# Attention scores turned by VectorE block transposes in place of TensorE transposes

## The chip, the cores and the metric

One Trainium2 chip, of which the kernel uses one core. The metric is the device time of the program in microseconds. Engines are named as in the profile: PE is TensorE (PEld its weight loads), DVE is VectorE, ACT is ScalarE, POOL is GpSimd, SP is the queue that issues the DMAs.

## The reference, cut to what matters

Three parts follow one another. Attention packs 576 keys of each of 64 heads (8 batches of 8 heads) into 32 vectors and lets 576 queries attend to them; a gated feed-forward layer with an RMS norm follows, then a second feed-forward layer with h·cos(h).

```python
def sm_attn(qq, kk, vv):
    s = scale * np.matmul(qq, kk.transpose(0, 1, 3, 2))
    s = s - np.max(s, axis=-1, keepdims=True)
    a = np.exp(s)
    a = a / (np.sum(a, axis=-1, keepdims=True) + 1e-09)
    return np.matmul(a, vv)
p_packed = sm_attn(p, k, v)              # 32 packed vectors of each head
out = sm_attn(q, p_packed, p_packed)     # 576 queries, 32 keys: the softmax that the change rebuilds
# then: x = rows (batch, position), 512 columns
xn = x / rms * rms_g
g = xn @ w_gate; x1 = (silu(g) * (xn @ w_val)) @ w_out     # d_ff 1536
h = x1 @ w_in;   y = (h * cos(h)) @ w2_out                 # d_ff 2048
```

All of it is float32. The kernel keeps the precision by splitting each operand of the large matmuls into a high and a low part (`hilo`) and adding three products (`mm3`).

## The kernel before, in words

**First stage.** A loop over i from 0 to 17 packs one group of four heads per pass: `u_prep`, `u_kt`, `u_s1`, `u_e`, `u_et`, `u_pp`, `u_fin`, while the weights are loaded and turned from 64-bit to 32-bit form (`narrow`: DVE lines 143 to 153 on tiles wy, ny). From pass 5 on the attention of batch 0 runs in it: `attend(0)` is a generator and `bg0_step` takes three of its steps per pass, until `ATT_U` steps are done.

**Blocks.** Then come eight blocks, one per batch b, of 24 iterations each (12 column groups f of the first feed-forward layer, two halves of the positions). An iteration is `gv_block` (12 matmuls into two PSUM tiles named gv), a step of attention, `acc_block` (6 matmuls into acc, for the iteration three before), another step of attention, and at six places `unit` (8 matmuls into mps, then `hilo`). `acc_block` has a place in its middle where only steps whose name begins with x are taken. In block b the steps of `attend(b+1)` are spread by `att_step`: `N_ATT` steps over the 48 half-iterations. So blocks 0 to 6 hold the attention of batches 1 to 7, and block 7 none. Block 0 also narrows the rest of the weights (`b0_step`), which loads DVE, ACT and POOL more than in later blocks.

**Attention of one batch before.** For each of two head groups g: query tiles (96 positions, 2 heads, 6 chunks) are transposed on PE three at a time into a PSUM tile qtp, ACT copies it to qT; after four of these, 8 matmuls give the scores sp, two tiles of 128 rows (4 heads by 32 keys) by 288 positions. ACT and DVE copy one each to sT, six PE transposes bring positions to the rows (stp, 96 rows), DVE takes the maximum over 32 keys and subtracts it into s. Then two exponentials on ACT (line 264), two sums, reciprocals and products on DVE (268 to 274). The steps named in `ATT_ORD` follow: t (three PE transposes into atp, ACT copies to at), x (matmuls xp with the packed vectors, squares for the norm on ACT, sums on DVE), r (rp, the root), b (the root is broadcast by three PE transposes into rb and multiplied into at), p (`hilo` into apt, the operand of `gv_block`).

**Order and buffers.** From the first stage until well into the last one the program order is the order in which the code is written (`manual_schedule`), on every engine. PSUM tiles of attention, `unit` and gv share one pool: two banks in the first stage, four in the blocks, taken in turn. An engine executes its instructions in order, so a wait holds all that stands behind it.

**Last stage.** The second feed-forward layer (`h_block`, `o_block`) has no attention in it; `o_out` stores the rows.

Of the kernel before, what the change touches and what calls it, by code (L numbers as in the profile page):

```python
# [20 lines left out]
def kernel(  # L21
# [14 lines left out]
    nc = tc.nc  # L36
    B, H, S, D = q.shape
    NP = p.shape[2]
# [3 lines left out]
    CP = 96  # L42
    NC_ = S // CP
    HALF = S // 2
    CH = NC_ // 2
# [7 lines left out]
    scale = 1.0 / math.sqrt(D)  # L53
# [30 lines left out]
    ATT_FROM, ATT_TO, ATT_FROM0, ATT_TO0, N_ATT = 0, 48, 10, 45, 37  # L84
    BX, BS, BW = 10, 13, 12

    wide = w_gate.dtype != F32
# [89 lines left out]
    psb = [ps_bg]  # L177
# [38 lines left out]
        nc.sync.dma_start(out=cl, in_=c_dram[b])  # L216

    def attend(b):
        s = a1.tile([CP, NC_, H, NP], F32, tag="s", name="s")
        for g in range(2):  # L220
            qTs = []
            for j in (2 * g, 2 * g + 1):
                qv = qn.pop(4 * b + j)
                qT = a2.tile([128, 2, HALF], F32, tag="qT", name="qT")
                for i in range(2):
                    tp = psb[0].tile([128, HALF], F32, tag="mm", name="qtp")
                    for c in range(CH):
                        nc.tensor.transpose(  # L228
                            tp[:, c * CP:(c + 1) * CP], qv[:, i, 2 * c:2 * c + 2, :].rearrange("p c d -> p (c d)"),
                            ident[:CP, :CP],  # L230
                        )
# [12 lines left out]
            sT = a1.tile([128, 2, HALF], F32, tag="sT", name="sT")  # L244
            nc.scalar.activation(out=sT[:, 0], in_=sp[0], func=AF.Copy)
            nc.vector.tensor_copy(sT[:, 1], sp[1])
            yield
            for r in range(2):
                st_p = psb[0].tile([CP, CH, 4, NP], F32, tag="mm", name="stp")
                for c in range(CH):  # L250
                    nc.tensor.transpose(
                        st_p[:, c].rearrange("p h n -> p (h n)"), sT[:, r, c * CP:(c + 1) * CP], ident
                    )
                mx = a2.tile([CP, CH, 4], F32, tag="amx", name="amx")
                nc.vector.tensor_reduce(out=mx, in_=st_p, op=ALU.max, axis=AX.X)
                nc.vector.tensor_tensor(
                    out=s.rearrange("p (c t) h n -> p c t h n", t=2)[:, :, r, 4 * g:4 * g + 4, :], in0=st_p,
                    in1=mx.unsqueeze(3).to_broadcast([CP, CH, 4, NP]), op=ALU.subtract,
                )
            yield  # L260
        n_s = 8 * CH
        hv = [s[:, hf * CH:(hf + 1) * CH].rearrange("p c h n -> p (c h) n") for hf in range(2)]
        for sf in hv:
            nc.scalar.activation(out=sf, in_=sf, func=AF.Exp, scale=scale)
            yield "e"
        for sf in hv:
            sm = a2.tile([CP, 2, n_s], F32, tag="sm", name="sm")
# [4 lines left out]
            if b:  # L272
                yield
            nc.vector.tensor_tensor(
                out=sf, in0=sf, in1=sm[:, 1].unsqueeze(2).to_broadcast([CP, n_s, NP]), op=ALU.mult
            )
            yield

        def transposed(hf, kt):
            tp = psb[0].tile([128, HALF], F32, tag="mm", name="atp")  # L280
            for c in range(CH):
                nc.tensor.transpose(
                    tp[:, c * CP:(c + 1) * CP],
                    s[:, hf * CH + c, 4 * kt:4 * kt + 4, :].rearrange("p h n -> p (h n)"), ident[:CP, :CP],
                )
            return tp

        z = {}

        def a_t(hf, kt):  # L290
            if (hf, kt) == (0, 0):
                z["at"] = a1.tile([128, 2, 2, HALF], F32, tag="at", name="at")
            nc.scalar.activation(out=z["at"][:, kt, hf], in_=transposed(hf, kt), func=AF.Copy)

        def a_x(kt, part):
            at = z["at"]
# [26 lines left out]
            )  # L323
            nc.gpsimd.tensor_tensor(out=ri[:, 1], in0=ri[:, 0], in1=mhalf, op=ALU.pow)

        def a_b(hf, _):
            at, ri = z["at"], z["ri"]
            rb = psb[0].tile([128, HALF], F32, tag="mm", name="rb")
            for c in range(CH):
                nc.tensor.transpose(  # L330
                    rb[:, c * CP:(c + 1) * CP], ri[:, 1, 2 * c + hf:2 * c + hf + 1].to_broadcast([CP, 128]),
                    ident[:CP, :CP],
                )
            nc.vector.tensor_tensor(
                out=at[:, :, hf], in0=at[:, :, hf], in1=rb.unsqueeze(1).to_broadcast([128, 2, HALF]), op=ALU.mult
            )

        def a_p(hf, _):
            ap = ap_t[b, hf] = a3p[0].tile([128, 2, 2, HALF], F32R, tag="apt", name="apt")
# [16 lines left out]
    st = {}  # L356
# [648 lines left out]
    def o_out(n, t):  # L1005
        if t % 2 == 0:
            ob_t[0] = pp_p.tile([128, 2, DM], F32, tag=f"pp{t // 2 % 2}", name="ob")
        ob = ob_t[0][:, t % 2]
        if t % 2:
            nc.vector.tensor_copy(ob, o_t[n][t])  # L1010
        else:
            nc.scalar.activation(out=ob, in_=o_t[n][t], func=AF.Copy)
        off = 0
        while off < 128:
            if n < B:
                b, u = n, t * 128 + off
# [64 lines left out]
```

## Time and profile before

| what | value |
|---|---|
| median of 3 runs | 1689.0 us (1687.13 to 1690.26) |
| span of the profiled execution | 1681.2 us |
| its own time | not listed; the runs lie 5.9 to 9.1 us above the span |
| PE busy | 1628.8 us, 97% of the span |
| DVE busy | 1008.5 us, 60% |
| ACT busy | 845.2 us, 50% |
| share of PE in the chain that ended last | 89% |

The span is the time from the first to the last instruction in the trace. A busy PE is not a PE at its peak, since its matmuls overlap; what an instruction costs on PE is read from the starts of the instructions beside it. The share over the whole span mixes stages with different limits, so the rows below are read by stretch.

### The profile page before, as it was taken

Reading aid. Unit: us, or ns where it says so; the run is one execution under the profiler, and the core shown is the slowest. Engines: PE = TensorE matmul, PEld = TensorE weight load, DVE = VectorE, ACT = ScalarE, POOL = GpSimd, SP = SyncE. Lnnn points to the kernel's source line nnn. Section 1 sums busy time; section 2 is a strip of 40 time slices with the busy share of each in tenths; the row PEclk is TensorE's granted clock in tenths of the full one; section 3 lists DMA queues with packets and bytes.
Section 4 is the critical chain, followed back from the end, with each engine's and each line's share of the span. In section 5 each row is a group of like instructions: output and inputs, shape, how many; then the busy total and the mean of one; then the engine's idle time right before and its main releaser. Section 6 shows DMA issues by size and latency. Waiting matters only on the chain.

```text
span 1681.2 us, 26128 instructions
## 1 busy us (share of the span) xinstructions
PE 1628.8 (97%) x10112; PEld 1325.8 (79%) x10112; DVE 1008.5 (60%) x1890; ACT 845.2 (50%) x1587; POOL 73.9 (4%) x74
## 2 busy tenths in 40 slices
PE   7877999999999999999999999999999999999998
PEld 5545868788888788888888888888888888888887
DVE  3577985566565666665435665656565656565554
ACT  4455555455454545454434554545454545454443
POOL 1001430000000000000110000000000000000000
PEclk9887999999999999999999999999999999999999
DMA  9996744454535454544363020101010101000001
GB/s 253 285 247 173 226 158 153 145 183 139 195 120 179 143 176 144 170 127 131 104 239 106 25 63 1 51 1 51 0 50 1 50 1 41 11 0 26 1 26 25
DMA packets 103580, 177.35 MB, mean 105 GB/s; under 512 B 39456, under 2 KB 55840, under 8 KB 103456
## 3 DMA queue, kind: packets, MB, share of 16 engines
q1 hardware_dynamic: 103456, 175.68, 34.4%
q8 instruction: 80, 1.31, 0.3%
q14 instruction: 44, 0.36, 0.1%
HBM read 134.22 MB, written 41.42 MB: 104 GB/s over the span
## 4 chain that ended last, share of the span: by engine, by line
PE 89%; DMA 5%; DVE 3%; ACT 1%; issue 1%; SPq 1%; POOL 0%; DVEq 0%; POOLq 0%; ACTq 0%
PE hp L160 8%; PE hp L159 8%; PE hp L158 8%; PE ops L160 8%; PE ops L159 8%; PE ops L158 8%; PE gv L158 6%; PE acc L158 6%; PE gv L159 6%; PE gv L160 6%; PE acc L160 6%; PE acc L159 6%; PE mps L580 3%; DMA kn<-in_k_dram 2%; PE qtp L228 1%
## 5 line engine op out<-in xcount | busy, mean ns | idle before, releaser
L158 PE MATMUL gv<-apt,wmhl 128*128 128x288 f32 x768 | 237.8, 310 | 3.0 <-DVE silu L766 2.0
L159 PE MATMUL gv<-apt,wmhl 128*128 128x288 f32 x768 | 228.6, 298 | 0.2 <-DVE apt L107 0.2
L160 PE MATMUL gv<-apt,wmhl 128*128 128x288 f32 x768 | 228.0, 297 | 0.0
L159 PE MATMUL hp<-xhl,wmhl 128*128 128x512 f32 x576 | 224.1, 389 | 0.0
L160 PE MATMUL hp<-xhl,wmhl 128*128 128x512 f32 x576 | 224.1, 389 | 0.0
L158 PE MATMUL ops<-w2hl,ghl 128*128 128x512 f32 x576 | 224.1, 389 | 0.0
L159 PE MATMUL ops<-w2hl,ghl 128*128 128x512 f32 x576 | 224.1, 389 | 0.0
L158 PE MATMUL hp<-xhl,wmhl 128*128 128x512 f32 x576 | 223.9, 389 | 0.0
L160 PE MATMUL ops<-w2hl,ghl 128*128 128x512 f32 x576 | 222.3, 389 | 0.0
L981 ACT ACTIVATE r<-r 128x512 f32<-128x512 f32 x144 | 91.1, 633 | 250.0 <-DVE r L980 250.0
L989 DVE TENSOR_TENSOR r<-r,hp 128x512 f32<-128x512 f32 x144 | 98.9, 687 | 164.8 <-ACT r L982 164.8
L158 PEld LDWEIGHTS gv<-apt,wmhl 128*128 128x128 f32 x768 | 146.0, 190 | 44.3 <-issue 17.6
L158 PE MATMUL acc<-shl,wohl 128*128 128x512 f32 x432 | 176.6, 409 | 0.2 <-DMA shl<-s 0.2
L160 PE MATMUL acc<-shl,wohl 128*128 128x512 f32 x432 | 170.7, 395 | 2.4 <-POOL wohl L546 2.4
L159 PE MATMUL acc<-shl,wohl 128*128 128x512 f32 x432 | 169.6, 393 | 0.0
L773 ACT ACTIVATE shl<-silu 128x288 fp32r<-128x288 f32 x192 | 85.4, 445 | 159.6 <-DVE silu L766 158.4
L766 DVE TENSOR_TENSOR silu<-silu,gv 128x288 f32<-128x288 f32 x192 | 86.5, 451 | 125.5 <-PE gv L160 106.2
L976 ACT ACTIVATE kk<-hp,magic 128x512 f32<-128x512 f32 x144 | 99.1, 688 | 117.3 <-PE hp L160 117.1
L159 PEld LDWEIGHTS gv<-apt,wmhl 128*128 128x128 f32 x768 | 146.2, 190 | 4.4 <-DVE apt L107 0.5
L160 PEld LDWEIGHTS gv<-apt,wmhl 128*128 128x128 f32 x768 | 145.8, 190 | 0.0
L977 DVE TENSOR_SCALAR kk<-kk 128x512 f32<-128x512 f32 x144 | 61.4, 426 | 116.1 <-ACT kk L976 116.0
L158 PEld LDWEIGHTS ops<-w2hl,ghl 128*128 128x128 f32 x576 | 108.2, 188 | 22.6
(127 smaller groups left out, 2708.4 us busy)
## 6 DMA issues: line engine op xcount, KB each, us to landing
wy<-wy SPq DMA_DIRECT2D x96, 512.0 KB, 4.5
kn<-in_k_dram SPq DMA_DIRECT2D x16, 576.0 KB, 7.4
vn<-in_v_dram SPq DMA_DIRECT2D x48, 192.0 KB, 6.5
qnat<-in_q_dram SPq DMA_DIRECT2D x32, 288.0 KB, 4.1
x_dram<-x SPq DMA_DIRECT2D x18, 512.0 KB, 3.0
x1raw<-x_dram SPq DMA_DIRECT2D x18, 512.0 KB, 4.0
raw<-in_moe_w_in_dram SPq DMA_DIRECT2D x16, 512.0 KB, 4.2
raw<-in_moe_w_out_dram SPq DMA_DIRECT2D x16, 512.0 KB, 4.2
```

The lines of the kernel that those rows point to most:

```text
L158: nc.tensor.matmul(ps, lhi, rhi, start=first, stop=False)
L159: nc.tensor.matmul(ps, lhi, rlo, start=False, stop=False)
L160: nc.tensor.matmul(ps, llo, rhi, start=False, stop=last)
L228: nc.tensor.transpose(tp[:, c * CP:(c + 1) * CP], qv[:, i, 2 * c:2 * c + 2, :].rearrange("p c d -> p (c d)"), ident[:CP, :CP],)
L580: nc.tensor.matmul(ps[kt][h * NP:(h + 1) * NP], ppT[b // 4][rows, 4 * kt + h, n:n + NP], w_y[2 * u + kt][rows, j], start=True, stop=True,)
L766: nc.vector.tensor_tensor(out=t, in0=t, in1=pss[1], op=ALU.mult)
L773: nc.scalar.activation(out=sh[:, 0, cols], in_=t, func=AF.Copy)
L976: nc.scalar.activation(out=kk, in_=hp, func=AF.Identity, scale=1.0 / TWO_PI, bias=magic[:, 0:1])
L977: nc.vector.tensor_scalar(out=kk, in0=kk, scalar1=-MAGIC, scalar2=None, op0=ALU.add)
L981: nc.scalar.activation(out=r, in_=r, func=AF.Abs)
L989: nc.vector.tensor_tensor(out=r, in0=r, in1=hp, op=ALU.mult)
```

## The change

The scores leave PSUM through two DVE instructions per head group that transpose blocks of 32 by 32 (`nc.vector.transpose`, STREAM_TRANSPOSE in the program). Since a head has 32 packed keys, this puts 32 positions of a head on 32 rows and its keys along the row; the softmax then works on 128 rows with 18 groups of 32. The copies to sT and the PE transposes stp are gone. The way back is one DVE block transpose of 128 by 576 for each half kt, in place of the PE transposes atp and their ACT copies. The exponential is one instruction instead of two. The query transposes of a head pair take two PSUM tiles in one step, and both broadcasts of the root stand in one step. There are fewer steps: 25 instead of 33 in batch 0, 27 instead of 37 in the others. The positions come out in another order, which the row addresses of the output undo.

```diff
-    ATT_U, U_ATT = 31, 5
+    ATT_U, U_ATT = 23, 5
-    ATT_ORD = "t00 t10 - x00 t01 t11 - x10 - - r00 - - b00 b10 p00 p10"
-    ATT_ORD0 = "t00 t10 x00 x01 t01 t11 x10 x11 - r00 - b00 b10 p00 p10"
+    ATT_ORD = "t00 - x00 t10 - x10 - - r00 - - b00 p00 p10"
+    ATT_ORD0 = "t00 x00 x01 t10 x10 x11 - r00 - b00 p00 p10"
...
+                tps = [psb[0].tile([128, HALF], F32, tag="mm", name="qtp") for _ in range(2)]
                 for i in range(2):
-                    tp = psb[0].tile([128, HALF], F32, tag="mm", name="qtp")
                     for c in range(CH):
...
-                    nc.scalar.activation(out=qT[:, i], in_=tp, func=AF.Copy)
+                for i in range(2):
+                    nc.scalar.activation(out=qT[:, i], in_=tps[i], func=AF.Copy)
                     qTs.append(qT[:, i])
-                    if i == 0:
-                        yield
...
-            sT = a1.tile([128, 2, HALF], F32, tag="sT", name="sT")
-            nc.scalar.activation(out=sT[:, 0], in_=sp[0], func=AF.Copy)
-            nc.vector.tensor_copy(sT[:, 1], sp[1])
+            st = a2.tile([128, 2, NB, NP], F32, tag="st", name="st", bufs=1)
+            for r in range(2):
+                nc.vector.transpose(st[:, r].rearrange("p c n -> p (c n)"), sp[r])
             yield
-            for r in range(2):
-                st_p = psb[0].tile([CP, CH, 4, NP], F32, tag="mm", name="stp")
-                for c in range(CH):
-                    nc.tensor.transpose(
...
+            mx = a2.tile([128, 2 * NB], F32, tag="amx", name="amx")
+            nc.vector.tensor_reduce(out=mx, in_=sv, op=ALU.max, axis=AX.X)
+            nc.vector.tensor_tensor(
+                out=s[:, g].rearrange("p r c n -> p (r c) n"), in0=sv,
...
-        for sf in hv:
-            nc.scalar.activation(out=sf, in_=sf, func=AF.Exp, scale=scale)
-            yield "e"
+        nc.scalar.activation(out=s, in_=s, func=AF.Exp, scale=scale)
+        yield "e"
...
-            nc.scalar.activation(out=z["at"][:, kt, hf], in_=transposed(hf, kt), func=AF.Copy)
+            nc.vector.transpose(
+                z["at"][:, kt].rearrange("p r x -> p (r x)"), s[:, kt].rearrange("p r c n -> p (r c n)")
+            )
...
+            rb = [psb[0].tile([128, HALF], F32, tag="mm", name="rb") for _ in range(2)]
...
+            c = 2 * (c % CH) + c // CH
```

The first place is PE in the first stage, in pass 7 of the loop; kp, pp and et belong to the packing. Before:

```order
L404 MATMUL kp<-ident,kn 128x128 x3
L241 MATMUL sp<-qT,bq 32x288 x8
L460 MATMUL pp<-vn,eT 32x64 x24
L251 MATMUL stp<-ident,sT 96x128 x6
L228 MATMUL qtp<-ident,qnat 128x96 x3
L446 MATMUL et<-ident,e 128x128 x6
```

The same pass now:

```order
L391 MATMUL kp<-ident,kn 128x128 x3
L229 MATMUL qtp<-ident,qnat 128x96 x6
L447 MATMUL pp<-vn,eT 32x64 x24
L229 MATMUL qtp<-ident,qnat 128x96 x6
L241 MATMUL sp<-qT,bq 32x288 x8
L433 MATMUL et<-ident,e 128x128 x6
```

The second scores now stand in this pass, two passes earlier than before, behind two query steps that use both banks each.

The second place is DVE late in the first stage, in pass 14, from the packed vectors ppT to the narrowing of a weight (ny); wmhl is the low half made by `unit`, ssq and ri belong to the norm of batch 0. Before:

```order
L479 TENSOR_TENSOR ppT_176<-tp,gT 128x4x32
L312 TENSOR_TENSOR ssq<-ssq,sq 128x288 x2
L464 TENSOR_SCALAR cd<-pp,mx 128x128
L107 TENSOR_TENSOR wmhl<-mps,wmhl 128x512 x2
L320 TENSOR_SCALAR ri<-rp 96x6
L143 TENSOR_SCALAR ny<-ny 128x512
```

The same pass now:

```order
L466 TENSOR_TENSOR ppT_176<-tp,gT 128x4x32
L451 TENSOR_SCALAR cd<-pp,mx 128x128
L107 TENSOR_TENSOR wmhl<-mps,wmhl 128x512 x2
L143 TENSOR_SCALAR ny<-ny 128x512
```

The sums and the root of batch 0 are gone from this pass: they stand in passes 11 and 12.

The third place is DVE in block 1, from the copy of x1 to the lower part shl of the next iteration; wmhl comes from `unit`. Before:

```order
L805 COPY x_3275<-acc 128x512
L107 TENSOR_TENSOR wmhl<-mps,wmhl 128x512 x2
L777 TENSOR_TENSOR shl<-silu,shl 128x288
L766 TENSOR_TENSOR silu<-silu,gv_3315 128x288
L246 COPY sT<-sp 128x288
L255 TENSOR_REDUCE amx<-stp 96x12
L256 TENSOR_TENSOR s<-stp,amx 96x3x128
L255 TENSOR_REDUCE amx<-stp 96x12
L256 TENSOR_TENSOR s<-stp,amx 96x3x128
L777 TENSOR_TENSOR shl<-silu,shl 128x288
```

And now:

```order
L792 COPY x_3200<-acc 128x512
L246 STREAM_TRANSPOSE st<-sp 128x288 x2
L107 TENSOR_TENSOR wmhl<-mps,wmhl 128x512 x2
L764 TENSOR_TENSOR shl<-silu,shl 128x288
L753 TENSOR_TENSOR silu<-silu,gv_3246 128x288
L250 TENSOR_REDUCE amx<-st 128x18
L251 TENSOR_TENSOR s<-st,amx 128x576
L764 TENSOR_TENSOR shl<-silu,shl 128x288
```

The two transposes stand one iteration earlier, and maximum and subtraction are one instruction each.

## Rows read from the trace of the kernel before

**Rows 1.** Windows: length, busy PE, PEld, DVE, ACT, POOL; clock, DMA share, GB/s.
```profile
0.00:154.00 154.00, 113.71 (x1468) 76.79 (x1468) 89.25 (x221) 75.24 (x182) 8.45 (x31) 0.87 0.93 249
154.00:264.00 110.00, 102.72 (x714) 82.17 (x715) 90.54 (x162) 60.00 (x129) 40.17 (x25) 0.95 0.57 179
440.00:528.00 88.00, 88.00 (x656) 72.00 (x653) 54.06 (x115) 45.79 (x97) 1.43 (x1) 1.00 0.50 162
873.00:1681.00 808.00, 803.60 (x3546) 665.07 (x3544) 473.04 (x769) 403.38 (x630) 5.07 (x4) 1.00 0.11 32
```

**Rows 2.** Timeline of PE in block 3: start, length, engine, line, operation.
```profile
450.66 0.41 PE L228 MATMUL qtp<-ident,qnat 96*128 96x96 f32 x3
450.86 0.48 PE L158 MATMUL acc<-shl,wohl 128*128 128x512 f32 x1
451.17 0.40 PE L159 MATMUL acc<-shl,wohl 128*128 128x512 f32 x1
...
460.46 0.40 PE L159 MATMUL acc<-shl,wohl 128*128 128x512 f32 x1
460.69 0.39 PE L160 MATMUL acc<-shl,wohl 128*128 128x512 f32 x1
460.92 0.82 PE L251 MATMUL stp<-ident,sT 128*96 128x128 f32 x6
461.49 0.38 PE L158 MATMUL gv<-apt,wmhl 128*128 128x288 f32 x1
461.71 0.30 PE L159 MATMUL gv<-apt,wmhl 128*128 128x288 f32 x1
461.84 0.29 PE L160 MATMUL gv<-apt,wmhl 128*128 128x288 f32 x1
```

**Rows 3.** Groups of PE in block 3: count | busy us, mean ns | idle before.
```profile
L282 PE MATMUL atp<-ident,s 96*128 96x96 f32 x12 | 1.6, 244 | 0.0
```

**Rows 4.** Chain of waits, the units at the ends of block 3: start, length.
```profile
440.25 1.02 PE mps L580 x16
...
528.22 1.02 PE mps L580 x16
```

**Rows 5.** Groups of DVE and ACT over the span, by shape.
```profile
L255 DVE TENSOR_REDUCE amx<-stp 96x12 f32<-96x384 f32 x32 | 17.6, 548 | 12.7 <-PE stp L251 12.7
L256 DVE TENSOR_TENSOR s<-stp,amx 96x384 f32<-96x384 f32 x32 | 17.7, 554 | 1.1
L274 DVE TENSOR_TENSOR s<-s,sm 96x768 f32<-96x768 f32 x16 | 15.2, 948 | 0.0
L246 DVE COPY sT<-sp 128x288 f32<-128x288 f32 x16 | 7.2, 451 | 1.0 <-PE sp L241 1.0
L334 DVE TENSOR_TENSOR at<-at,rb 128x576 f32<-128x576 f32 x16 | 11.7, 749 | 0.0
L143 DVE TENSOR_SCALAR ny<-ny 128x512 f32<-128x512 f32 x36 | 15.1, 419 | 0.0
L264 ACT ACTIVATE s<-s 96x768 f32<-96x768 f32 x16 | 13.5, 846 | 3.0 <-DVE s L256 2.9
```

**Rows 6.** Waits of PE from 160 to 264 us: total us, times, longest.
```profile
PE acc L160 <- POOL wohl L546: 2.4, 4, 0.6
PE gv L158 <- DVE silu L766: 2.0, 1, 2.0
PE atp L282 <- ACT silu L765: 1.3, 1, 1.3
```

**Rows 7.** Timeline of DVE late in the first stage: in brackets the wait before.
```profile
119.75 0.46 DVE L312 TENSOR_TENSOR ssq<-ssq,sq 128x288 f32<-128x288 f32 x1 [3.21 <-ACT sq L311]
...
130.19 1.02 DVE L312 TENSOR_TENSOR ssq<-ssq,sq 128x288 f32<-128x288 f32 x2 [3.55 <-ACT sq L311]
...
148.44 1.42 DVE L334 TENSOR_TENSOR at<-at,rb 128x576 f32<-128x576 f32 x2
```

**Rows 8.** Waits of the DMA queue SP in the first 165 us.
```profile
SPq L207 <- PE qtp L228: 2.5, 1, 2.5
```

More of the change, by code (lines that the diff above doesn't have):

```diff
@@ L79 @@
     LAG, LAG_B = 3, 4
-    ATT_ORD = "t00 t10 - x00 t01 t11 - x10 - - r00 - - b00 b10 p00 p10"
-    ATT_ORD0 = "t00 t10 x00 x01 t01 t11 x10 x11 - r00 - b00 b10 p00 p10"
+    ATT_ORD = "t00 - x00 t10 - x10 - - r00 - - b00 p00 p10"
+    ATT_ORD0 = "t00 x00 x01 t10 x10 x11 - r00 - b00 p00 p10"
     AL_AT, CL_AT = 16, 21
-    ATT_FROM, ATT_TO, ATT_FROM0, ATT_TO0, N_ATT = 0, 48, 10, 45, 37
+    ATT_FROM, ATT_TO, ATT_FROM0, ATT_TO0, N_ATT = 0, 48, 10, 45, 27
     BX, BS, BW = 10, 13, 12
@@ L218, in attend @@
     def attend(b):
-        s = a1.tile([CP, NC_, H, NP], F32, tag="s", name="s")
+        NB = HALF // NP
+        s = a1.tile([128, 2, 2, NB, NP], F32, tag="s", name="s")
         for g in range(2):
@@ L243, in attend @@
                     )
-            sT = a1.tile([128, 2, HALF], F32, tag="sT", name="sT")
-            nc.scalar.activation(out=sT[:, 0], in_=sp[0], func=AF.Copy)
-            nc.vector.tensor_copy(sT[:, 1], sp[1])
+            st = a2.tile([128, 2, NB, NP], F32, tag="st", name="st", bufs=1)
+            for r in range(2):
+                nc.vector.transpose(st[:, r].rearrange("p c n -> p (c n)"), sp[r])
             yield
-            for r in range(2):
-                st_p = psb[0].tile([CP, CH, 4, NP], F32, tag="mm", name="stp")
-                for c in range(CH):
-                    nc.tensor.transpose(
[L252 to L259, printed above, removed]
-            yield
-        n_s = 8 * CH
-        hv = [s[:, hf * CH:(hf + 1) * CH].rearrange("p c h n -> p (c h) n") for hf in range(2)]
-        for sf in hv:
-            nc.scalar.activation(out=sf, in_=sf, func=AF.Exp, scale=scale)
-            yield "e"
-        for sf in hv:
-            sm = a2.tile([CP, 2, n_s], F32, tag="sm", name="sm")
+            sv = st.rearrange("p r c n -> p (r c) n")
+            mx = a2.tile([128, 2 * NB], F32, tag="amx", name="amx")
+            nc.vector.tensor_reduce(out=mx, in_=sv, op=ALU.max, axis=AX.X)
+            nc.vector.tensor_tensor(
+                out=s[:, g].rearrange("p r c n -> p (r c) n"), in0=sv,
+                in1=mx.unsqueeze(2).to_broadcast([128, 2 * NB, NP]), op=ALU.subtract,
+            )
+            yield
+        nc.scalar.activation(out=s, in_=s, func=AF.Exp, scale=scale)
+        yield "e"
+        for g in range(2):
+            sf = s[:, g].rearrange("p r c n -> p (r c) n")
+            sm = a2.tile([128, 2, 2 * NB], F32, tag="sm", name="sm")
             nc.vector.tensor_reduce(out=sm[:, 0], in_=sf, op=ALU.add, axis=AX.X)
@@ L271, in attend, with a_t @@
             yield
-            if b:
-                yield
             nc.vector.tensor_tensor(
-                out=sf, in0=sf, in1=sm[:, 1].unsqueeze(2).to_broadcast([CP, n_s, NP]), op=ALU.mult
+                out=sf, in0=sf, in1=sm[:, 1].unsqueeze(2).to_broadcast([128, 2 * NB, NP]), op=ALU.mult
             )
             yield
[L279 to L286, printed above, removed]
         z = {}
-        def a_t(hf, kt):
-            if (hf, kt) == (0, 0):
+        def a_t(kt, _):
+            if kt == 0:
                 z["at"] = a1.tile([128, 2, 2, HALF], F32, tag="at", name="at")
-            nc.scalar.activation(out=z["at"][:, kt, hf], in_=transposed(hf, kt), func=AF.Copy)
+            nc.vector.transpose(
+                z["at"][:, kt].rearrange("p r x -> p (r x)"), s[:, kt].rearrange("p r c n -> p (r c n)")
+            )
         def a_x(kt, part):
@@ L324, in a_r, with a_b @@
             nc.gpsimd.tensor_tensor(out=ri[:, 1], in0=ri[:, 0], in1=mhalf, op=ALU.pow)
-        def a_b(hf, _):
+        def a_b(*_):
             at, ri = z["at"], z["ri"]
[L328 to L332, printed above, removed]
-                )
-            nc.vector.tensor_tensor(
-                out=at[:, :, hf], in0=at[:, :, hf], in1=rb.unsqueeze(1).to_broadcast([128, 2, HALF]), op=ALU.mult
-            )
+            rb = [psb[0].tile([128, HALF], F32, tag="mm", name="rb") for _ in range(2)]
+            for hf in range(2):
+                for c in range(CH):
+                    nc.tensor.transpose(
+                        rb[hf][:, c * CP:(c + 1) * CP],
+                        ri[:, 1, 2 * c + hf:2 * c + hf + 1].to_broadcast([CP, 128]), ident[:CP, :CP],
+                    )
+            for hf in range(2):
+                nc.vector.tensor_tensor(
+                    out=at[:, :, hf], in0=at[:, :, hf], in1=rb[hf].unsqueeze(1).to_broadcast([128, 2, HALF]),
+                    op=ALU.mult,
+                )
         def a_p(hf, _):
```

4 lines of the change are left out of this document (2 added, 2 removed).

## Prediction

> **What bounds the kernel now.** I read the windows by stage first, since the mean over the span hides that the stages differ [rows 1]. The first 154 us are bound by transfers and by a chain across engines: DMA share 0.93, PE busy 113.7 of 154 us at a mean granted clock of 0.87. Block 0 (154 to 264 us) is mixed: PE 102.7 of 110 us, DVE 90.5, POOL 40.2. Blocks 1 to 6 are all like block 3: PE busy 88.00 of 88.00 us, clock 1.00 (2.4 GHz), DVE 54.1, ACT 45.8. There PE alone sets the time, so an instruction taken from PE is worth exactly the distance it puts between its neighbours' starts, and one added to DVE or ACT is free as long as PE does not wait for it. The last 808 us contain nothing of the change.
>
> Then I read single instructions on PE, by their starts, because busy times overlap [rows 2]. Then the costs of the DVE and ACT shapes that stand nearest to the new ones [rows 5], then who PE waits for in block 0 [rows 6], and last the chain late in the first stage [rows 7] and the DMA queue [rows 8].
>
> **Blocks 1 to 6, PE.** An ordinary distance from acc to the next start is 0.23 us (460.46 to 460.69) and from gv to gv 0.13 (461.71 to 461.84). With six stp between, acc to gv is 460.69 to 461.49, so 0.80, which is 0.57 more; the gv after it takes 0.22, which is 0.09 more. A group of stp thus costs 0.66 us, and a block has two, one for each head group: 1.32 us. Three qtp cost 0.20 (450.66 to 450.86) and make the acc behind them 0.31 instead of 0.23, together 0.28 [rows 2]. The atp have the same shape and nearly the same length (244 ns [rows 3]); a block has four groups: 1.12 us. Of the 0.28, some 0.19 belong to the three instructions and 0.09 to the change of kind behind them, which is paid once per group. The eight qtp groups become four of double length, 0.47 instead of 0.56 each: 0.36 us. The two rb groups become one: 0.09 us. Sum 2.89 us a block, for six blocks 17.3 us.
>
> Does PE wait for anything new there? The order rows of block 1 show the tightest place: sp, then mps (1.02 us [rows 4]), then gv, which takes the first of the two banks that DVE reads for its transposes. DVE must be done with the first transpose about 1.0 us after sp ends and with the second 0.8 us later. At 0.45 us each that holds; from about 0.9 us each it becomes tight. The transposes at go from buffer to buffer two half-iterations before the x step, so nobody waits for them at these lengths.
>
> **What DVE and ACT pay.** No row shows a STREAM_TRANSPOSE. For 128x288 out of PSUM the nearest row is the copy of the same shape, 451 ns; for 128x576 the nearest is 749 ns (line 334) [rows 5]. The lower bound is the rate of line 143, 512 columns in 419 ns, which makes 0.24 and 0.47 us. Above, I see no row that bounds it; filling a block and emptying it one after the other would double the price, 0.90 and 1.50 us, and that is my upper end (an estimate). I take the copy's price, as the row of the same shape and source.
> DVE per batch: gone are two copies (0.90), four maxima (2.19), four subtractions (2.22) and two sums and two products, which I take at the product's 0.95 (3.79), together 9.10 us. New are four transposes (1.80), two (1.50), and two each of maximum, subtraction, sum and product of 576 columns at 0.75 (6.00), together 9.30 us. So DVE is left as it was, +0.2 us, and between −1.4 and +3.5 us with the bounds. In blocks 1 to 6 DVE has 34 us free, so none of this counts. ACT loses two sT copies, four at copies and one pair of table changes, and does one exponential of 1152 columns for two of 768 at 846 ns each. That exponential is at most the 1.69 us of the two and delays one silu by up to 0.85 us; the banks of gv are taken again two iterations later, and one iteration is 12 times 0.13 and 6 times 0.23 us [rows 2], 3.0 us, so I cost this at nothing. If that cover were gone, it would be 0.85 us a block.
>
> *A rule of the skill beside this.* The Trainium skill, Vector Engine (DVE) Microarchitecture Reference, section 3.8, says that the transposing array is pipelined to sustain one element per cycle and lane. By it the transposes cost what the copies cost, and the sum stays; by my upper end block 0 and the first stage would lose up to 3.3 us each. No run here shows it yet, so I keep the doubled price in the range.
>
> **Block 0.** PE can save the same 2.89 us at most. But PE waits here 2.0 us for DVE's silu product, 1.3 us for ACT and 2.4 us for the weight halves of POOL [rows 6], and DVE is busy for 82% [rows 1]. Where PE arrives earlier at a wait, the wait grows. The POOL waits follow a unit directly and keep their length; the one on DVE stands behind the softmax steps, after about 1.7 us of the saving (two stp groups and the query pairs), and eats part of it. I take half, 1.5 us; bounds 0 and 3, and a loss of 3 with slow transposes.
>
> **First stage.** The DVE work is as large as before, so what can go is its waiting. Three waits belong to the late steps of batch 0: 3.21 and 3.55 us for squares that need atp, a copy and xp one after the other, and 1.42 us for the products with the root that stand in the last pass [rows 7]. These steps move up to passes 10 to 13, and the copy on ACT is gone. On the other side passes 6, 8, 10 and 11 get denser: in passes 10 and 11 the four squares now come in two rounds through two banks each, which I price at 2 to 3 us a pass; passes 6 to 8 lie where the transfers bind and cost little. Moving the waits gives about −8 us in passes 12 to 15, the denser ones give +5: I take −3 us. Bounds: −8 (all of the waits, the denser passes hidden behind transfers) and +4 (the reverse, with the queue of [rows 8]).
>
> **Sum.** 17.3 + 1.5 + 3 = 21.8 us. The profiled execution spans 1681.2 us, so its span would be about 1659.4; the runs lie 5.9 to 9.1 us above that span, with the median 7.8 above, and nothing outside the span changes. 1689.0 − 21.8 = 1667.2, so 1667 us.
>
> **Rivals.**
> 1. *The first stage gets longer.* In pass 7 PE now runs two query steps and the scores through the same two banks, each waiting for copies of the step before. Two query loads stand behind the second query step on the in-order DMA queue, which already waited 2.5 us for such a step [rows 8], and the loads of v, k and weights stand behind them. Against it: loads of k are issued four passes ahead. Price +4 us: 1689.0 − 17.3 − 1.5 + 4 = 1674 us.
> 2. *The first stage gains its whole waits.* −8 us there and 3 in block 0: 1689.0 − 17.3 − 3 − 8 = 1661 us. For it: passes 14 and 15 now hold no attention at all. Against: the DVE instructions still have to be done in passes that were busy.
> 3. *TensorE's clock falls in the first stage.* The granted clock there is already 0.87 on average [rows 1], between its levels of 2.4 and 1.2 GHz, after stretches in which PE stood idle. Taking 24 transposes out gives it more idle time. If it cost the 3 us that the stage gains and 5 more, the sum would be 1689.0 − 17.3 − 1.5 + 5 = 1675 us. In blocks 1 to 6 PE has no gaps, so nothing falls there. The Trainium skill, TensorE: Matmul & The Clock Gate, section "HAM oscillation — how this bites in real kernels", describes a kernel that lost time in just this way, by gaps between bursts of matmuls; here the trace shows a low clock only in the first stage and early in block 0.
> 4. *Slower: the block transposes on float32 are several times a copy.* At four times, the six of a batch take 13.2 us instead of 3.3. The first stage and block 0, where DVE is in the chain, would pay 9.9 each; in blocks 1 to 6 a pair at sp holds its banks and DVE for 3.6 us against an iteration of 3.0 us, so PE waits about 0.6 us twelve times, 7 us. 1667 + 19.8 + 7 = 1694 us. It decides from about 3.8 times the copy's price. Against it: no DVE row of these sizes lies over 0.95 us.
>
> **How the numbers follow.** Forecast 63%, rival 1 15%, rival 2 12%, rival 3 5%, rival 4 5%. The forecast's own terms give 17.3 in all cases, block 0 from −3 to 3 and the first stage from −4 to 8: 1661 to 1679 at the corners. The range 1658 to 1677 takes in rivals 1, 2 and 3 and leaves out rival 4 and both far corners, under 2 in 10. A measurement of this kernel tells about 0.2% (3.4 us) from no change. Faster by more than that 93%; within it 2%, a rival 4 at about 3.8 times; slower 5%.
>
> **What would show it.** Blocks: the distance from one mps to the same mps a block later, 87.97 us before [rows 4], would be 85.1 us, with PE still busy for the whole of it and the clock at 1.00. DVE: st near 0.45 us, the transposes at near 0.75 us, DVE busy about 54 us a block. First stage: the end of the stage, the window edge of 154 us, at about 151 us, with no wait for squares after pass 12. I am wrong if PE in blocks 1 to 6 shows waits for st or at, if the transposes take over 0.9 us, or if the first gv starts later than before.

## The result, and the profile after

The changed kernel takes 1667.6 us (median of four runs, 1664.8 to 1671.4), the kernel before 1688.1 in the same comparison (four runs, 1686.4 to 1690.3): ratio 0.9879, 95% interval 0.9861 to 0.9898. A second comparison gave 0.9883 (0.9863 to 0.9903). 1667 us was forecast. The sum was right, but two of its terms were not: the first stage gained nearly three times what I gave it, and blocks 1 to 6 only two thirds of theirs. The experiments below are about these two.

The windows of the changed kernel, columns as in [rows 1]; the first two edges are its own (the first gv starts at 150.11 us, not 154.74), the third window is one block.

```profile
0.00:150.11 150.11, 107.28 (x1445) 71.93 (x1445) 88.90 (x223) 73.84 (x177) 8.54 (x31) 0.87 1.00 255
150.11:260.00 109.89, 102.87 (x724) 80.28 (x724) 91.30 (x162) 57.08 (x122) 39.33 (x25) 0.96 0.58 182
430.00:516.00 86.00, 85.74 (x630) 69.82 (x629) 54.44 (x115) 40.81 (x89) 1.74 (x1) 1.00 0.51 161
```

VectorE is as busy as before in each of them (88.90, 91.30 and 54.44 us against 89.25, 90.54 and 54.06), the DMA share of the first stage is 1.00 instead of 0.93, and PE in a block is no longer busy throughout: 85.74 of 86.00 us. That small gap is the first sign of a new wait.

The chain of waits, units of blocks 3 and 4 (start, length), answers to [rows 4]:

```profile
431.47 0.86 PE mps L567 x16
...
517.48 0.86 PE mps L567 x16
```

From one to the next are 86.01 us. It was 87.97, and 85.1 was forecast: the block gains 1.96 us, not 2.89.

The groups of VectorE and ScalarE over the span, by shape, answer to [rows 5]:

```profile
L246 DVE STREAM_TRANSPOSE st<-sp 128x288 f32<-128x288 f32 x32 | 13.6, 461 | 8.7 <-PE sp L241 8.7
L275 DVE STREAM_TRANSPOSE at<-s 128x576 f32<-128x576 f32 x16 | 12.3, 770 | 0.0
L251 DVE TENSOR_TENSOR s<-st,amx 128x576 f32<-128x576 f32 x16 | 12.1, 758 | 0.5
L256 ACT ACTIVATE s<-s 128x1152 f32<-128x1152 f32 x8 | 9.3, 1167 | 0.2
```

A block transpose of 288 columns takes 461 ns where the copy of that shape took 451 [rows 5], one of 576 columns 770 ns where 749 was the nearest row. The copy's price was the right one. The exponential takes 1.17 us, under the bound of 1.69. The Trainium skill (Vector Engine (DVE) Microarchitecture Reference, section 3.8) says that the transposing array sustains one element per cycle and lane. The trace agrees as far as it goes: a block transpose takes as long as the copy or the product of its shape.

**Where a block's gain went.** I took the distances from the first gv of an iteration to the first gv of the next out of the timeline of PE, in block 4 (the one whose iteration 2 ends with the unit at 517.48 us), and added them up by the steps they contain:

| steps of the block | before, us | changed, us | gain | forecast |
|---|---|---|---|---|
| queries and scores (qtp, sp, stp), iterations 0 to 8 | 34.5 | 32.7 | 1.8 | 1.68 |
| way back and x steps (atp, xp, rp), 13 to 20 | 29.8 | 29.3 | 0.4 | 1.12 |
| roots (rb), 21 to 23 | 10.7 | 10.9 | −0.2 | 0.09 |

The scores paid what was forecast. The −0.2 of the roots stands in block 4 alone, where iteration 22 takes 3.88 us; in the other five blocks it takes 3.60, and the roots gain 0.06. The way back did not pay, and one iteration explains it. In the kernel before, the second x step of block 4 takes 0.74 us and stands ahead of a unit (timeline of PE):

```profile
586.06 0.74 PE L302 MATMUL xp<-at,cl 32*64 32x288 f32 x16
587.62 1.09 PE L580 MATMUL mps<-wy,ppT 64*32 64x512 f32 x16
```

Timeline of PE in block 4 of the changed kernel: the first x step, and then, behind a unit, the second one:

```profile
557.86 0.74 PE L286 MATMUL xp<-at,cl 32*64 32x288 f32 x16
558.53 0.50 PE L158 MATMUL acc<-shl,wohl 128*128 128x512 f32 x1
...
562.40 1.09 PE L567 MATMUL mps<-wy,ppT 64*32 64x512 f32 x16
...
565.91 1.43 PE L286 MATMUL xp<-at,cl 32*64 32x288 f32 x16
567.27 0.50 PE L158 MATMUL acc<-shl,wohl 128*128 128x512 f32 x1
```

The same group of matmuls (eight in the program, which the profile lists as 16) lasts 0.74 us once and 1.43 us the other time. The second step stands in iteration 16, right behind the unit of iteration 15; before it stood in iteration 18, ahead of a unit. An x step takes all four banks of the pool, and the last of them is held by this iteration's second gv until VectorE has made the silu product. Timeline of VectorE at the same place:

```profile
564.21 1.29 DVE L107 TENSOR_TENSOR wmhl<-mps,wmhl 128x512 fp32r<-128x512 f32 x2 [1.46 <-ACT wmhl L106]
565.41 0.42 DVE L145 TENSOR_SCALAR ny<-ny 128x512 int32<-128x512 int32 x1
565.75 0.45 DVE L764 TENSOR_TENSOR shl<-silu,shl 128x288 fp32r<-128x288 f32 x1
566.11 0.45 DVE L753 TENSOR_TENSOR silu<-silu,gv 128x288 f32<-128x288 f32 x1
```

The product (line 753) starts at 566.11, behind two halves of the unit's weights, a step of the background conversion ny and the half of the previous product. The x step began at 565.91 and gets its last bank when the product is done. In other blocks a longer step of ny stands there; this is block 3:

```profile
479.41 0.68 DVE L149 SCALAR_TENSOR_TENSOR ny<-raw,ny 128x512 int32<-128x512 int32 x1
480.01 0.45 DVE L764 TENSOR_TENSOR shl<-silu,shl 128x288 fp32r<-128x288 f32 x1
```

In the three blocks where ny takes 0.42 us the x step's iteration is 4.65 us, in the three where it takes 0.68 it is 4.92 or 4.93. The iteration of the first x step is 3.85 us in all six. So PE waits 0.80 or 1.07 us a block, 5.6 us in six blocks. The waits listed for PE say little of this (0.8 us in three places), because the wait lies inside a group of 16 and shows as a longer group.

### The profile page after: what moved, and what is told of

Same layout as the page of the kernel before. It is cut to its first block, busy times and chain, and to the rows that moved or that the text cites. A ratio compares the mean times of both kernels' runs of the same rounds, so it can differ in the third digit from the quotient of the medians.

```text
span 1664.0 us, 25652 instructions
## 1 busy us (share of the span) xinstructions
PE 1608.4 (97%) x9920; PEld 1306.0 (78%) x9920; DVE 1005.7 (60%) x1890; ACT 807.0 (48%) x1519; POOL 74.1 (4%) x74
## 4 chain that ended last, share of the span: by engine, by line
PE 87%; DVE 5%; DMA 3%; ACT 2%; issue 1%; POOL 1%; SPq 0%; DVEq 0%; ACTq 0%; POOLq 0%
PE ops L160 8%; PE ops L158 8%; PE hp L160 8%; PE hp L158 8%; PE ops L159 8%; PE hp L159 8%; PE gv L158 6%; PE acc L158 6%; PE acc L160 6%; PE gv L159 5%; PE acc L159 5%; PE gv L160 5%; PE mps L567 3%; DMA kn<-in_k_dram 2%; PE xp L286 1%
## 5 line engine op out<-in xcount | busy, mean ns | idle before, releaser
L760 ACT ACTIVATE shl<-silu 128x288 fp32r<-128x288 f32 x192 | 85.4, 445 | 212.6 <-DVE silu L753 211.2
L963 ACT ACTIVATE kk<-hp,magic 128x512 f32<-128x512 f32 x144 | 99.1, 688 | 117.4 <-PE hp L160 117.2
L159 PEld LDWEIGHTS hp<-xhl,wmhl 128*128 128x128 f32 x576 | 108.1, 188 | 22.6
```

Source lines behind the costliest of these rows:

```text
L159: nc.tensor.matmul(ps, lhi, rlo, start=False, stop=False)
L760: nc.scalar.activation(out=sh[:, 0, cols], in_=t, func=AF.Copy)
L963: nc.scalar.activation(out=kk, in_=hp, func=AF.Identity, scale=1.0 / TWO_PI, bias=magic[:, 0:1])
```

## The experiments

All times are medians; a ratio is to the kernel before, with its 95% interval. Runs of one kernel spread over some 6 us, and the profiles show where much of that can come from: pass 7 of the first stage (a pass begins with its first et) starts at 64.9 us in one and at 72.1 in another, of kernels that are alike up to there. Distances inside the blocks repeat within 0.1 us, so the blocks are compared by these. "Unit to unit" below is the distance from the unit of iteration 21 of a block to that of the next, for blocks 1 to 6.

**The changed kernel again.** 

> The changed kernel once more, unaltered, so that the next three runs have it beside them on the same chip. Both theories expect what was seen: about 0.988 of the time of before, blocks 86.0 us from mps to mps, and the second x step of a block (the 16 xp behind the unit at iteration 15) with an iteration of 4.65 to 4.95 us, where the first x step has one of 3.85 us.

Measured: 1668.2 us, ratio 0.9883 (0.9863 to 0.9903). The distances from unit to unit of five blocks are 86.23, 86.05, 85.74, 86.04 and 86.20 us; the x step's iteration 4.65 or 4.93, as in the first trace.

**The second x step one iteration later.**

```diff
-    ATT_ORD = "t00 - x00 t10 - x10 - - r00 - - b00 p00 p10"
+    ATT_ORD = "t00 - x00 t10 - - x10 - r00 - - b00 p00 p10"
```

> The changed kernel, with the second x step moved one iteration later (17 instead of 16), so that it no longer stands in the iteration right behind a unit. Nothing else moves. Theory A: the part of the block's gain that is missing (2.89 predicted, 1.9 measured) is PE waiting inside the second x step for its four banks, because VectorE has the two halves of the unit's weights before the silu product that frees a bank. Then the x step's iteration falls from 4.65 to 4.95 to about 3.85 us, a block from 86.0 to about 85.1 us, and the whole by 6 x 0.94 = 5.6 us against the changed kernel. Theory B: the cover is short because VectorE's block transposes and the one long exponential delay the products wherever the x step stands. Then the wait moves along, and the time stays within 1.5 us of the changed kernel.

Measured: 1660.7 us, ratio 0.9847 (0.9824 to 0.9871). Unit to unit 85.23, 85.09, 85.09, 85.36 and 85.25 us: 0.85 less on average. Timeline of PE in block 4 of this kernel:

```profile
565.67 0.74 PE L286 MATMUL xp<-at,cl 32*64 32x288 f32 x16
```

And what VectorE does just ahead of it:

```profile
563.88 0.45 DVE L764 TENSOR_TENSOR shl<-silu,shl 128x288 fp32r<-128x288 f32 x1
565.15 0.46 DVE L753 TENSOR_TENSOR silu<-silu,gv 128x288 f32<-128x288 f32 x1 [0.82 <-PE gv L160]
```

Now VectorE waits for gv (0.82 us), not PE for VectorE, and the x step is 0.74 us again. Theory A holds, B falls: the transposes and the exponential are unchanged here. The way back in block 4 now takes 28.6 us and so gains 1.1 against before: the 1.12 that the prediction had for it. The median falls by 7.5 us, and the two intervals overlap a little; 0.85 us for six blocks are 5.1 of these, and the rest is within the spread of the runs.

**The mirror: the kernel before, with its second x step behind the unit.**

```diff
-    ATT_ORD = "t00 t10 - x00 t01 t11 - x10 - - r00 - - b00 b10 p00 p10"
+    ATT_ORD = "t00 t10 t01 x00 t11 x10 - - - - r00 - - b00 b10 p00 p10"
```

> The kernel before (TensorE transposes, single query steps), with only its second x step brought forward to the iteration right behind the unit at 15, where the changed kernel has it; the transposes t01, t11 that it needs come forward with it. Theory A (the place behind the unit costs it): PE waits there in this kernel too, 0.8 to 1.07 us a block, and it gets slower than before by 6 x 0.94 = 5.6 us, ratio about 1.0033. Theory B (VectorE's transposes or the exponential cause it): this kernel has none of them there, and stays within 1.5 us of before.

Measured: 1690.6 us, ratio 1.0013 (1.0000 to 1.0025). Timeline of PE in block 4 of this kernel, both x steps and the unit between them:

```profile
581.10 0.74 PE L302 MATMUL xp<-at,cl 32*64 32x288 f32 x16
582.67 1.09 PE L580 MATMUL mps<-wy,ppT 64*32 64x512 f32 x16
585.38 0.41 PE L282 MATMUL atp<-ident,s 96*128 96x96 f32 x3
586.45 1.16 PE L302 MATMUL xp<-at,cl 32*64 32x288 f32 x16
```

The wait is there in a kernel that has no block transpose: 1.16 against 0.74 us, and 88.31 to 88.63 us from unit to unit instead of 87.95. So the place makes it. Its size, 0.36 to 0.68 us a block, 3.1 us in six, is smaller than the 5.6 expected. Here a group of atp stands between the gv and the x step in the same iteration, and what PE does in that time (0.28 us) it need not wait. I had taken the price from the changed kernel without counting that. It is the larger part of the 0.4 us a block that are missing; where the rest went is open.

**One VectorE step less behind the unit.**

```diff
-            if not w2_skip[0]:
+            if not w2_skip[0] and not (b and j == 15):
```

> The changed kernel, with the second x step where it was (iteration 16), and one step of the background weight conversion (ny, one VectorE instruction of 0.42 or 0.68 us that stands between the two halves of the unit's weights and the silu product) taken out of that one place in each block and done an iteration later, with all that follow it. Theory A (PE waits in the x step for the product on VectorE, and for nothing else): in the trace of the changed kernel the iteration is 4.65 us where ny is 0.42 and 4.93 where it is 0.68, so without it 4.31 in all six blocks, 0.34 or 0.61 us less each, and 2.8 us less in all. Rival (ACT's silu behind its two weight halves, or the banks of the unit, set the wait): the iteration stays at 4.65 or more.

Measured: 1664.0 us, ratio 0.9866 (0.9838 to 0.9895). Timeline of VectorE in block 3:

```profile
476.88 0.45 DVE L764 TENSOR_TENSOR shl<-silu,shl 128x288 fp32r<-128x288 f32 x1
477.24 0.45 DVE L753 TENSOR_TENSOR silu<-silu,gv 128x288 f32<-128x288 f32 x1
```

and of PE:

```profile
477.37 1.10 PE L286 MATMUL xp<-at,cl 32*64 32x288 f32 x16
```

All six blocks have the iteration at 4.32 us (expected 4.31), and unit to unit are 85.43 or 85.67 us. Without ny the wait shrinks by what ny took on VectorE from its start to the next (0.34 or 0.60 us). The banks of the unit and the silu on ScalarE were left as they were, so neither set that part of the wait. The 0.47 us that remain (4.32 against 3.85) were not taken apart by a run of their own; VectorE goes from the halves of the weights, which start at 475.67, to the product without a gap. Some comes back: the iteration of the roots, which stands behind the unit of iteration 21, is 3.88 us in blocks 2, 4 and 6 and 3.62 in the others, where the changed kernel has 3.88 in block 4 alone; the steps of ny have moved by one.

**Roots ahead of their unit as well.**

```diff
-    ATT_ORD = "t00 - x00 t10 - - x10 - r00 - - b00 p00 p10"
+    ATT_ORD = "t00 - x00 t10 - - x10 - r00 - b00 - p00 p10"
```

> The second x step at iteration 17 as in the run with that alone, and the root broadcasts rb at iteration 21 ahead of the unit instead of 22 behind it. Theory A, which puts every wait on the place behind a unit: rb's iteration goes from 3.60 to about 3.47 us, the two banks now being free, so 6 x 0.13 = 0.8 us more than the x step alone; the roots have 1.5 iterations instead of 2.5 to be ready in, 4.4 us for a reduction and a power on GpSimd. Theory B: the same as with the x step alone, within 0.5 us. A third way: the root is not ready after 1.5 iterations, and PE waits for GpSimd at each rb, some 1 us a block, 6 us slower than the x step alone.

Measured: 1659.7 us, ratio 0.9835 (0.9813 to 0.9856), the lowest median of all, though within the noise of the run with the x step alone. Unit to unit 85.12, 85.08, 85.08, 85.08 and 85.15 us. Against the x step alone that is 0.1 us a block on average: 0.28 in the distance that holds the roots' iteration of 3.88 us, about 0.1 in two others and 0.01 in the other two. So theory A was too high with 0.13 in each block. The root was ready in time. 85.08 is 87.97 − 2.89, the sum of the prediction for a block.

**The first stage: the x steps off the unit there too.** Applied to the kernel above:

```diff
-    ATT_U, U_ATT = 23, 5
+    ATT_U, U_ATT = 25, 5
-    ATT_ORD0 = "t00 x00 x01 t10 x10 x11 - r00 - b00 p00 p10"
+    ATT_ORD0 = "t00 - - x00 x01 t10 x10 x11 - r00 - b00 p00 p10"
```

> The kernel with the second x step at 17 and the roots at 21, and now the steps of batch 0 in the first stage shifted too: the x steps of the first head group go from pass 10, where they stand right behind a unit, to pass 11, those of the second to pass 12, the roots to pass 13. Theory A (an x step right behind a unit waits for the banks that VectorE's halves of the unit's weights free, here of a pool of two banks): pass 10, 15.9 us in the changed kernel against 8.6 us before, loses the 3.6 us wait of PE and the two rounds of squares, some 7 us; pass 11 and 12 take 2 to 3 us of that back for the rounds. The stretch from the start of pass 10 to the first gv (56.7 to 58.3 us in four runs with these steps) becomes 52 to 55 us. Rival: the transfers bind these passes (DMA share 1.06 in pass 10), so the same stretch stays within 1 us of 57.

Measured: 1663.6 us, ratio 0.9863 (0.9847 to 0.9879). First the windows of the changed kernel (the first profile) for pass 10, for passes 11 to 13, and from there to the first gv; then of this kernel for pass 10, 11, 12 and the rest (columns as in [rows 1]):

```profile
93.24:109.13 15.89, 10.73 (x113) 5.45 (x113) 10.87 (x25) 7.23 (x17) 0.24 (x1) 0.88 1.06 295
109.13:129.82 20.69, 17.17 (x274) 11.39 (x271) 16.71 (x43) 12.81 (x33) 2.28 (x3) 0.84 0.82 219
129.82:150.11 20.29, 12.41 (x225) 7.55 (x225) 15.81 (x41) 12.02 (x29) 0.00 (x0) 0.82 0.98 282
```

```profile
93.65:102.54 8.89, 8.10 (x97) 5.25 (x98) 8.51 (x21) 4.14 (x11) 0.45 (x1) 0.81 1.08 276
102.54:113.33 10.79, 6.28 (x98) 3.50 (x98) 6.58 (x17) 6.44 (x16) 0.24 (x1) 0.92 1.06 326
113.33:123.05 9.72, 8.13 (x100) 4.85 (x98) 6.34 (x16) 5.73 (x14) 0.00 (x0) 0.68 0.88 193
123.05:151.62 28.57, 19.35 (x320) 13.12 (x317) 21.78 (x55) 15.84 (x38) 1.54 (x2) 0.84 0.79 229
```

Pass 10 does lose its 7 us (15.89 to 8.89), but the stretch from the start of pass 10 to the first gv stays: 57.97 us, where the five profiles with the changed kernel's steps there have 56.7 to 58.8. So theory A explains the pass, and not the stage: the stretch does what the rival said. The rival's reason, that the transfers bind, is not shown. The loads come earlier here: the second and third groups of loads of v are issued 9.1 and 15.4 us after the start of pass 10, in the changed kernel 12.0 and 21.3. What gets longer are passes 11, 12 and 13, by 1.9, 3.2 and 2.9 us, into which the x steps and the roots moved. In pass 11 PE now waits as long as it did in pass 10 of the changed kernel, where it was 3.6 us for wmhl (waits of PE in pass 11 of this kernel):

```profile
PE xp L286 <- ACT ssq L292: 3.7, 1, 3.7
```

The steps took their wait along.

**Block 0: the x steps an iteration later.** `ATT_FROM0, ATT_TO0` from 10, 45 to 12, 47, on top of the last.

> As the run before it, and the steps of batch 1 in block 0 one iteration later, so that the x steps stand in iterations 16 and 18, ahead of a unit in the same iteration, instead of 15 and 17, behind one. Theory A: the iterations of the x steps, 5.3 and 5.3 us now, fall by 0.7 to 1.0 us each, so block 0 gets 1.4 to 2 us shorter. Rival: block 0 has a unit in every second iteration and VectorE busy for four fifths of it, so any place waits, and block 0 stays within 0.5 us.

Measured: 1665.2 us, ratio 0.9874 (0.9853 to 0.9895). From the first gv to the start of iteration 24 it takes 99.4 us, where the kernel above it takes 98.1: 1.3 us longer. Theory A fails here. By iterations the trace gives: 5 to 12, where the queries and scores stand, 0.7 us longer; 13 to 16, with the first x step, 0.3 shorter; 17 and 18, with the second one, 0.4 longer; 19 to 23, with the roots, 0.5 longer. So the loss stands at the other steps that moved along, not at the first x step. The granted clock differs too: here it is 0.50 from 210.8 to 217.6 us, within iterations 15 and 16, and 1.00 in these iterations of the kernel above. What that cost is not known; iterations 13 to 16 are shorter all the same.

**Batch 0 late, as before.** In the changed kernel:

```diff
-    ATT_U, U_ATT = 23, 5
+    ATT_U, U_ATT = 31, 5
-    ATT_ORD0 = "t00 x00 x01 t10 x10 x11 - r00 - b00 p00 p10"
+    ATT_ORD0 = "- - - - - - - t00 - x00 x01 - t10 x10 x11 - r00 - b00 p00 p10"
```

> The changed kernel with the late steps of batch 0 put back into the passes where the kernel before had them (x steps in passes 13 and 14, the reduction in 15, the roots after the last pass), everything else as in the changed kernel. From the start of pass 10 to the first gv the kernel before took 64.3 us (two runs), the changed one 56.7 to 58.3 (four runs). Theory A (the first stage gained 6 to 8 us because the steps moved up, out of a stretch where x steps stood behind the unit of pass 14 and the products with the root behind the last pass): it goes back to 62 to 65 us, and the whole is 5 to 7 us slower than the changed kernel. Theory B (it gained by the work that is gone: 24 PE transposes, a stage of copies): it stays at 57 to 59 us. The blocks are those of the changed kernel, 86.0 us.

Measured: 1673.9 us, ratio 0.9919 (0.9891 to 0.9947). From pass 10 to the first gv 61.7 us: between the 57.7 of the changed kernel (mean of five profiles) and the 64.3 before. Neither theory alone: of the 6.6 us that this stretch gained, about 4 come from where the steps stand, and about 2.6 from the rest of the change. The place works both ways: from pass 12 to the first gv this kernel takes 43.6 us, the kernel before 44.4 and the changed one 32.1; passes 10 and 11 take 18.0, 19.8 and 24.8. Block 0, which is built as in the changed kernel, takes 99.5 us instead of 98.0, so that the stretch and the block together grow by 5.4 us; by the medians it is 5.7. The windows of pass 14 and of what follows it, first of the kernel before, then of this one:

```profile
129.58:143.66 14.08, 9.15 (x115) 5.21 (x112) 9.12 (x21) 6.07 (x15) 0.00 (x0) 0.66 0.69 195
143.66:154.74 11.08, 7.01 (x135) 4.85 (x135) 9.07 (x24) 6.16 (x15) 1.45 (x1) 0.81 0.63 182
```

```profile
130.09:144.13 14.04, 10.42 (x116) 5.28 (x114) 9.77 (x22) 6.29 (x15) 0.00 (x0) 0.74 0.80 211
144.13:157.77 13.64, 8.96 (x142) 6.28 (x139) 9.87 (x26) 6.96 (x17) 1.34 (x1) 0.63 0.62 171
```

Pass 14 is 14 us in both: the x steps stand at its unit, the passes have few transfers (share 0.6 to 0.8), and nothing hides the waits. In the changed kernel the long wait is in pass 10, where the transfers are busy (1.06). That they hide it there was not shown: pass 10 became 7.3 us longer.

**The block transposes four times, and twice.** Each `nc.vector.transpose` in a loop of 4, or of 2, to the same destination.

> The changed kernel with each of VectorE's block transposes issued four times in place of once, to the same destination: 18 more instructions a batch, 12 of 0.46 and 6 of 0.77 us, so 10.1 us more of VectorE a batch. This is the price that the slow rival of the prediction assumed (1694 us in all). By its working the first stage and block 0 pay up to 9.9 us each, and the blocks 1.2 us each, since the scores' banks are held for 3.7 us. By the theory that the blocks have VectorE time to spare, but not behind a unit, the two score steps of a block (the second directly ahead of its unit, and the gv after it takes their banks) pay 1 to 2 us each and the x steps nothing: blocks 88 to 90 us in place of 86.0, first stage and block 0 some 5 us each, in all 1668 + 12 to 24 + 10, about 1690 to 1702 us.

> The changed kernel with each block transpose issued twice. With four times, the time rose by 47.6 us, 5.7 us a block. The prediction had the blocks pay nothing below about 2 times the copy's price (0.9 us each, tight at sp ahead of the unit and the gv) and the first stage and block 0 at most 3.3 us each: 1668 + 3 to 7, 1671 to 1675. If the cost is in proportion to the instructions added, a third of 47.6: 1684 us, with the blocks at 87.9. If the blocks have a first part free, as the cover of one iteration suggests, they are below 87.0, and the whole lies at 1674 to 1680.

Measured: four times 1715.8 us, ratio 1.0164 (1.0138 to 1.0190); twice 1678.2 us, 0.9936 (0.9917 to 0.9956). Unit to unit 89.9 to 91.9 us with four, 86.5 to 86.7 with two, against 86.05. Waits of PE over four blocks (total us, times, longest), with four, and then with two:

```profile
PE gv L158 <- DVE st L247: 8.0, 8, 1.4
PE gv L158 <- ACT silu L754: 2.2, 4, 0.6
PE xp L288 <- DVE silu L755: 2.0, 4, 0.6
```

```profile
PE gv L158 <- DVE st L247: 1.5, 4, 0.4
```

The gv behind the unit waits for the bank that VectorE still reads: the tight place that the prediction named. Twice costs 0.6 us a block, 2.4 in block 0 (100.4 against 98.0) and 3.7 in the first stage from pass 7 on: 10 us in all, what was expected of a partly covered cost. Four times costs 47.6 us, 14 more than the upper end of what I expected: 5.3 us a block on average (32 in six), 6.7 in block 0 and 9.5 in the first stage. In most blocks 3.7 us of it stand in iterations 2 and 3, 0.8 in iteration 7 and about 1.1 in iteration 16 with the second x step, where I expected nothing. I had left out that the units' weights and the products queue behind the eight transposes on VectorE, so that one step's delay is handed to the next. A straight line between the two (an estimate) puts the point at which the change would no longer pay at about 2.5 times the present price.

## Why the prediction was right, and where two errors cancelled

- **Blocks 1 to 6, forecast 17.3 us, measured 11.5.** The prices were right: queries and scores gained 1.8 us against 1.68, and with the x step out of the way a block is 85.08 us. The step that failed is "Does PE wait for anything new there?". I looked for waits for what the change adds (st, at) and named sp, mps, gv; that place held. I did not ask where the shorter list of steps puts the steps that did not change. The second x step went from iteration 18, ahead of a unit, to 16, behind one, and waits there 0.80 or 1.07 us for VectorE. Moving it away gives 5.1 us back, moving ny away 0.34 or 0.61 a block, and moving it there in the kernel before costs that kernel 0.4 to 0.7 a block: that cause is shown.
- **Block 0, forecast 1.5 us, measured 1.2** (99.1 to 98.0 us from the first gv to iteration 24), within its bounds. The waits that were to eat half of the gain are still there; waits of PE from 155 to 264 us, which answer to [rows 6] (the last 16 us are block 1, to which one of the five in the first row belongs):

```profile
PE acc L160 <- POOL wohl L533: 2.5, 5, 0.6
PE acc L159 <- DVE shl L764: 2.3, 1, 2.3
PE acc L158 <- ACT wohl L530: 1.2, 2, 0.9
```

  They are as long as before (2.4, 2.0 and 1.3 us), and the one on VectorE has moved from gv to acc. The starts of the iterations show the gain being eaten where they stand: iterations 0 to 12 are 1.4 us shorter than before, 13 to 16 are 0.6 longer, 17 to 23 are 0.4 shorter. No run took these waits away.
- **First stage, forecast 3 us, measured about 8.7 in its later part.** From pass 10 to the first gv it went from 64.3 us (two profiles) to 57.7 (five), and passes 7 to 9 from 26.1 or 26.3 us to 24.0 in all five. The end of the stage moved only by 4.6 us from the first profile before to the first after, because pass 7 began 4.8 us later in the second; by the means of the same profiles, two and five, it moved by 8.3 (156.9 to 148.5). This is the size that rival 2 had, which I gave 12%, but not its way: it had the denser passes hidden. The mis-sized term is "−8 us in passes 12 to 15": passes 12 to the first gv went from 44.4 us to 32.1 in the two first profiles, −12.3. The denser passes cost what was forecast, +5: pass 10 +7.3, pass 11 −2.3. The some 2 us of passes 7 to 9 were in no term; they are gained with batch 0 late as well (24.0 us), and their cause is open. The windows, first of the kernel before for pass 10 and from pass 12 to the first gv, then of the changed one from pass 12 on (pass 10 is above):

```profile
90.49:99.12 8.63, 7.49 (x99) 4.24 (x97) 8.02 (x19) 3.46 (x9) 0.51 (x1) 1.00 1.03 284
110.33:154.74 44.41, 31.03 (x440) 19.25 (x440) 29.82 (x76) 24.27 (x60) 1.45 (x1) 0.77 0.67 185
```

```profile
118.03:150.11 32.08, 22.68 (x402) 14.91 (x399) 25.64 (x67) 19.62 (x48) 2.28 (x3) 0.83 0.93 254
```

  In the profile of before I counted only the waits of VectorE [rows 7]. Those of PE in pass 14 lay beside them unread; this is the list of the kernel before for that pass:

```profile
PE mps L580 <- ACT sq L311: 3.5, 1, 3.5
PEld rp L318 <- DVE wmhl L107: 3.2, 1, 3.2
```

  As forecast, VectorE no longer waits for squares after pass 12.
- **The sum.** 11.5 + 1.2 + 8.7 = 21.4 us from the stretches, 18.8 to 20.5 by the medians, 21.8 forecast. The blocks missed 5.8 us and the first stage brought 5.7 more than forecast. That these cancel is luck.
- **Rival 1** (first stage longer) is excluded by the stretches above. **Rival 3** (clock): the granted clock of the first stage is 0.87 before and after, so no loss by it shows there. The prediction saw a low clock only there and early in block 0. There is one more stretch of 3.4 us at 1.2 GHz in the middle of block 0, before (212.6 to 216.0 us) and after (200.9 to 204.3). With the x step and the roots moved it is absent, and iterations 13 to 16 take the same 21.6 us as in the changed kernel. With batch 0 late there are two such stretches, from 209.3 and from 219.5 us, after waits of PE of 2.3 us and of 0.9 and 0.6; there these iterations take 23.1 us, in a block that is built alike. The loss that the Trainium skill describes (TensorE: Matmul & The Clock Gate, section "HAM oscillation — how this bites in real kernels") may show in these 1.5 us; no run tested it. **Rival 4** (transposes several times a copy): 461 ns against 451 excludes it. Its price was too low: at four times 1715.8 us, not 1694, and the change would lose from about 2.5 times on, not from 3.8.
- **Two slips in the working**, on which no term rests. With the lower bound the transposes save 1.4 us a batch, so VectorE would stand at −1.2, not −1.4. Of the two corners, 1661 and 1679 us, the range leaves out only the second.

## What to carry to other kernels

When a change shortens a list of steps that is spread over iterations, look up where every step lands that did not change: here one that takes all banks of a pool moved behind a unit and lost a third of the gain. A wait inside a group of equal instructions appears as a longer group, not in the list of waits, so compare a group's length with that of its twin elsewhere. And in the first stage a wait taken out of one pass came back in the passes to which its steps moved; a stage has to be judged by its end, over several profiles.

## What was not expected of the hardware

The start of pass 7 lay between 64.9 and 72.1 us over the eight profiles of kernels that are alike up to there, so one profile of this first stage says little about a gain of 3 us. And a block transpose of float32 costs what a copy does (461 against 451 ns for 288 columns out of PSUM): turning by VectorE was as cheap here as evicting.
